# A decode transformer block on Trainium2: the first load issued as two halves of 64 partitions, from two engines

## The chip, the cores and the metric

The kernel runs on one core of one Trainium2 chip. The metric is the device time of one execution in microseconds; the number given is the median of several runs.

## The reference

Four sequences, one new token each (B = 4, D = 448), go through one block: layer norm, attention over a cache, output projection, residual; then layer norm twice, an MLP (448 to 1792 to 448, tanh GELU) and a second residual. Everything is float32.

```python
q = (layernorm(x) @ wq)                     # 16 heads of 256
k, v = caches[:, :, 4096 - 1024:, :]        # 8 kv heads, last 1024 positions, each used by 2 heads
p = softmax(q @ k.T * 256 ** -0.5)
h = x + (p @ v) @ wo
y = layernorm(layernorm(h))
out = h + gelu(y @ w1 + b1) @ w2 + b2
```

## The kernel before, in words

The work on the cache is split into eight groups, one per kv head. Of each group the kernel needs the query weights (128 rows by 1792 floats once packed), the keys and the values (128 by 8192 floats each), and the output weights (128 by 1792). Nearly all bytes are used once, so the kernel is a stream of large loads through two rings of two buffers each, with the compute behind them.

**Ring "k"** holds the keys of a group and, in the same load, the query weights of the next group. **Ring "v"** holds the values of a group and its output weights. The very first load is different: it takes a buffer of ring "v" for the query weights of group 0 together with `xT`, the token `x` transposed to 128 partitions by 4 chunks by 4 sequences (16 floats per partition). In all it is 1808 floats in each of 128 partitions, 904 KB. The second load (`k0`, line 69) is the keys of group 0 and three quarters of the query weights of group 1; the last quarter of those comes as two small transfers (`wq1_last`, line 73). After that come, in this order, keys 1, values 0, keys 2, values 1 and so on, and at the end the MLP weights `w1` and `w2` through ring "k".

All these loads are issued by SyncE (SP), from the helper `load` (line 48; the DMA is line 52). ScalarE issues four small DMAs (line 132): the rows of `x`, `b1` and `b2` in another layout, 11 KB in all as the profile counts them. They write the tile `rs`, which GpSimd clears first (line 130), behind its clearing of `qT`, `oT`, `pT` and `gT` (line 127).

**The path from the first load.** TensorE takes column means of `xT` (lines 138 and 139), VectorE centres it (148) and squares it (268), TensorE and VectorE take the variance (138, 139, 141, 152), GpSimd the power -0.5 (153), VectorE writes the normed token `yT` (271 to 273), TensorE projects it with the query weights of group 0 (159), ScalarE copies the result (161), TensorE transposes it (165), VectorE folds it (167) and writes `qT` (173). Then `scores` of group 0 can start on the keys (182). Later steps on the same engines: VectorE maxima (186), ScalarE exponentials (194), TensorE transposes of the probabilities (207), values (219), the transposed output (240) and its sum over groups in `acc` (248).

**What sets the order.** TensorE's instructions run in the order of the program text. Those of the other engines are put in order by a scheduler at build time, which also places the waits: a load into a ring's buffer waits until the last reader of the buffer's former contents is done. Completions of loads are counted on eight counters, handed to the loads in the scheduler's order, so each load also waits for the landing of the load that had its counter eight loads earlier.

Of the kernel before, what the change touches and what calls it, by code (L numbers as in the profile page):

```python
# [8 lines left out]
F32 = mybir.dt.float32  # L9
# [6 lines left out]
B, D = 4, 448  # L16
# [4 lines left out]
P = 128  # L21
H = P // 2
ND = 4
# [4 lines left out]
CACHE = NKC * B * DH  # L28
WEIGHTS = 4 * D
# [4 lines left out]
def block_kernel(ctx: ExitStack, tc, rows, wq0, k0, wq1, kq, vo, w1, w2, out):  # L34
    nc = tc.nc
    const = ctx.enter_context(tc.tile_pool(name="const", bufs=1))
    ring = ctx.enter_context(tc.tile_pool(name="ring", bufs=2))
# [10 lines left out]
    def load(kind, src, pieces, name):  # L48
        t = ring.tile([P, CACHE + WEIGHTS], F32, tag=kind, name=name)
        at = 0  # L50
        for n in pieces:
            nc.sync.dma_start(t[:, at : at + n], src[:, at : at + n])  # L52
            at += n
        return t


    def wq_parts(t, last=None):
        parts = [(a, yT[:, a, :], slice(0, 512), t[:, a * 512 : (a + 1) * 512]) for a in range(3)]
        if last is not None:
            return parts + [(3, yT[:H, 3, :], slice(0, 512), last)]  # L60
        for i in range(2):
            parts.append((3, yT[:, 3 + i, :], slice(i * 2 * P, (i + 1) * 2 * P), t[:, 3 * 512 :]))
        return parts
# [195 lines left out]
        return pool.tile([P, 2, DH], F32, tag=tag, name=f"po{g}")  # L259


    t = load("v", wq0, (WEIGHTS + ND * B,), "wq0")
    wqt = wq_parts(t[:, :WEIGHTS])
    xT = t[:, WEIGHTS : WEIGHTS + ND * B].rearrange("p (a b) -> p a b", a=ND)
    d = work.tile([P, ND, B], F32, tag="d", name="d_x")
# [31 lines left out]
    t = load("k", w1, (2 * F, F + F // 2), "w1")  # L297
    w1t = [t[:, a * F : min((a + 1) * F, 3 * F + F // 2)] for a in range(ND)]
    t = load("k", w2, (8 * D, 4 * D, 2 * D), "w2")
# [127 lines left out]
    for c in range(first, NFC):  # L427
        for j in range(4):
            m, n = (Q, 2) if c == first else (B, 2 if j < 3 else 1)
# [75 lines left out]
```

## Time and profile before

| | us |
|---|---|
| median of 3 runs | 214.59 (214.48 to 214.62) |
| span of the profiled execution, first to last instruction | 212.9 |
| median less span | 1.69 |

The profile gives a span but no device time of its own for the profiled execution, so the median stands for it: 1.69 us lie outside the span, before the first or after the last instruction. Columns of the profile's tables are explained where its lines are shown. PE is TensorE, PEld its weight loads, DVE VectorE, ACT ScalarE, POOL GpSimd, SP SyncE; a q behind an engine's name is its DMA issuing. L52 is line 52 of the kernel. A row such as `0.73 0.39 SPq L52` gives start and duration in microseconds from the span's start.

### The profile page before, as it was taken

The numbers are of one execution on the slowest core, as the hardware profiler recorded it, in microseconds if no ns is written. First come the engines' busy times: TensorE is split into PE (matmuls) and PEld (weight loads), VectorE is DVE, ScalarE is ACT, GpSimd is POOL, SyncE is SP. The second block draws the span as 40 slices with busy tenths as digits, with TensorE's granted clock in tenths as the row PEclk, the third lists the DMA queues.
The fourth block names the chain that finished last, engine by engine and source line by source line (L and its number), as shares of the span: only waits on it lengthen the run. The fifth ranks groups of instructions, "written<-read, shape, count | busy, mean of one in ns | idle before, by whom it ended". The sixth has DMA issues, their size and how long they took to land.

```text
span 212.9 us, 2306 instructions
## 1 busy us (share of the span) xinstructions
PE 137.9 (65%) x971; PEld 49.1 (23%) x971; DVE 39.2 (18%) x167; ACT 21.0 (10%) x52; POOL 5.6 (3%) x17
## 2 busy tenths in 40 slices
PE   0456868093886739583986348382948476798994
PEld 0322233021231212211231113120222123234432
DVE  1420324001130202210130104110230231022320
ACT  0210213000030000300030003000030001000311
POOL 6100000000000000000000000000000000000110
PEclk9999999669597966969599859979797999699999
DMA  7999998999989999999999999999989999999991
GB/s 291 426 399 469 398 465 378 459 465 390 458 378 465 465 390 458 398 446 465 390 458 405 443 465 386 465 413 428 461 375 468 440 428 390 417 418 433 424 390 60
DMA packets 3865, 88.46 MB, mean 415 GB/s; under 512 B 448, under 2 KB 576, under 8 KB 1168
## 3 DMA queue, kind: packets, MB, share of 16 engines
q1 hardware_dynamic: 3824, 88.29, 96.9%
q8 instruction: 7, 0.11, 0.2%
q10 hardware_dynamic: 32, 0.05, 0.1%
q14 instruction: 2, 0.02, 0.0%
HBM read 88.26 MB, written 0.07 MB: 415 GB/s over the span
## 4 chain that ended last, share of the span: by engine, by line
DMA 85%; PE 11%; DVE 2%; issue 0%; SPq 0%
DMA v<-vo 65%; DMA w<-w 12%; DMA k<-k 8%; PE po L219 8%; PE acc L248 1%; DVE o L236 1%; PE pot L240 1%; PE py L431 1%; DVE oT L243 0%; DVE oT L244 0%; SPq L52 0%; DVE res L437 0%; PE py L256 0%
## 5 line engine op out<-in xcount | busy, mean ns | idle before, releaser
L182 PE MATMUL s<-k,qT 128*32 128x512 f32 x256 | 42.3, 822 | 24.7 <-DMA k<-kq 22.6
L219 PE MATMUL po<-v,pT 128*32 128x512 f32 x256 | 40.0, 772 | 19.6 <-DMA v<-vo 19.6
L186 DVE TENSOR_REDUCE mx<-s 128x1 f32<-128x512 f32 x16 | 11.1, 691 | 67.4 <-PE s L182 67.4
L182 PEld LDWEIGHTS s<-k,qT 128*32 128x32 f32 x256 | 10.0, 146 | 54.7 <-issue 29.4
L219 PEld LDWEIGHTS po<-v,pT 128*32 128x32 f32 x256 | 10.7, 135 | 42.3 <-issue 31.4
L161 ACT COPY qs<-pq 128x512 f32<-128x512 f32 x8 | 4.7, 586 | 135.8 <-PE pq L159 135.8
L236 DVE TENSOR_SCALAR o<-po,rec 128x512 f32<-128x512 f32 x8 | 6.0, 750 | 60.2 <-PE po L219 60.2
L194 ACT ACTIVATE p<-s,nm 128x512 f32<-128x512 f32 x16 | 10.9, 690 | 18.4 <-DVE nm L190 18.4
L207 PE MATMUL ppt<-ident,p 128*128 128x128 f32 x64 | 10.5, 286 | 2.0 <-ACT p L194 1.7
L165 PE MATMUL pqt<-ident,qs 128*128 128x128 f32 x32 | 5.7, 304 | 6.2 <-ACT qs L161 6.2
L240 PE MATMUL pot<-ident,o 128*128 128x128 f32 x32 | 5.2, 286 | 5.7 <-DVE o L236 5.7
L248 PE MATMUL acc<-v,oT 128*32 128x448 f32 x56 | 6.7, 551 | 3.3 <-DVE oT L244 3.3
L207 PEld LDWEIGHTS ppt<-ident,p 128*128 128x128 f32 x64 | 6.7, 140 | 6.0 <-ACT p L194 6.0
L159 PE MATMUL pq<-k,yT 128*32 128x512 f32 (+1 forms) x66 | 7.3, 515 | 0.0
L308 PE MATMUL warm<-idle 128*32 128x512 bf16 x25 | 7.3, 382 | 0.0
L240 PEld LDWEIGHTS pot<-ident,o 128*128 128x128 f32 x32 | 3.3, 140 | 13.0 <-DVE o L236 13.0
L165 PEld LDWEIGHTS pqt<-ident,qs 128*128 128x128 f32 x32 | 3.6, 150 | 10.9 <-ACT qs L161 9.1
L153 POOL TENSOR_TENSOR r<-ve_r,mhalf 128x1 f32<-128x1 f32 x2 | 1.1, 544 | 191.9 <-DVE ve_r L152 191.9
L211 DVE COPY pT<-ppt 128x16 f32<-128x16 f32 x32 | 4.7, 170 | 4.7 <-PE ppt L207 4.7
L159 PEld LDWEIGHTS pq<-k,yT 128*32 128x32 f32 x66 | 3.1, 110 | 6.1 <-issue 4.8
L138 PE MATMUL pm_x<-wq,mean 128*128 128x12 f32 x2 | 0.6, 363 | 5.8 <-DMA wq<-wq 5.8
L167 DVE TENSOR_REDUCE sm<-pqt 128x16 f32<-128x64 f32 x8 | 1.8, 225 | 13.0 <-PE pqt L165 13.0
(101 smaller groups left out, 60.9 us busy)
## 6 DMA issues: line engine op xcount, KB each, us to landing
v<-vo SPq DMA_DIRECT2D x7, 4992.0 KB, 31.8
k<-kq SPq DMA_DIRECT2D x6, 4992.0 KB, 32.0
k<-k SPq DMA_DIRECT2D x1, 4864.0 KB, 16.3
k<-kq SPq DMA_DIRECT2D x1, 4096.0 KB
w<-w SPq DMA_DIRECT2D x2, 1792.0 KB
v<-vo SPq DMA_DIRECT2D x2, 1024.0 KB, 22.2
v<-vo SPq DMA_DIRECT2D x1, 2048.0 KB
w<-w SPq DMA_DIRECT2D x1, 1344.0 KB
```

The costliest lines, as they stand in the source:

```text
L159: nc.tensor.matmul(pq[j * Q : (j + 1) * Q, cols], y, w, start=True, stop=True)
L161: nc.scalar.copy(qs, pq)
L165: nc.tensor.transpose(pt[:, i, :], qs[:, i * P : (i + 1) * P], ident)
L182: nc.tensor.matmul(s[b * Q : (b + 1) * Q, :], qT[g % 2][:, c, b, :], kt[h][:, c, b, :], start=(c == 0), stop=(c == 1),)
L186: nc.vector.reduce_max(mx[:, h : h + 1], s, axis=AX.X)
L194: nc.scalar.activation(p[:, h * 512 : (h + 1) * 512], halves[h], AF.Exp, bias=nm, scale=SCALE, accum_out=sums[:, h : h + 1],)
L207: nc.tensor.transpose(pt[:, c, :], p[:, (4 * h + c) * P : (4 * h + c + 1) * P], ident)
L219: nc.tensor.matmul(po[b * Q : (b + 1) * Q], pT[g % 2][:, c, b, :], vt[c][:, :, b, :], start=(c == 0), stop=(c == NKC // 2 - 1),)
L236: nc.vector.tensor_scalar_mul(o, po, rec)
L240: nc.tensor.transpose(pt[:, i, c], o[:, i, c * P : (c + 1) * P], ident)
L248: nc.tensor.matmul(acc[i * Q : (i + 1) * Q, :], oT[g % 2][:, i, :], wt[:, i, :], start=(g == 0), stop=(g == HKV - 2),)
L308: nc.tensor.matmul(warm[:Q], idle[:, :Q], idle, start=True, stop=True)
```

## The change

The first load no longer goes through `load`. Its tile is taken from ring "v" as before, and its 1808 columns are loaded in two DMAs: partitions 0 to 63 issued by SyncE, partitions 64 to 127 issued by ScalarE. Nothing else differs in the text.

```diff
-    t = load("v", wq0, (WEIGHTS + ND * B,), "wq0")
+    t = ring.tile([P, CACHE + WEIGHTS], F32, tag="v", name="wq0")
+    n = WEIGHTS + ND * B
+    for q, rows_half in ((nc.sync, slice(0, H)), (nc.scalar, slice(H, P))):
+        q.dma_start(t[rows_half, :n], wq0[rows_half, :])
     wqt = wq_parts(t[:, :WEIGHTS])
```

Here `P` is 128, `H` 64, `WEIGHTS` 1792, `ND * B` 16.

## The prediction

> **What bounds the kernel now.** I first read the top of the page: the span, the busy slices, the queues, the chain.
>
> ```profile
> span 212.9 us, 2306 instructions
> ...
> DMA  7999998999989999999999999999989999999991
> ...
> q1 hardware_dynamic: 3824, 88.29, 96.9%
> ...
> HBM read 88.26 MB, written 0.07 MB: 415 GB/s over the span
> ...
> DMA 85%; PE 11%; DVE 2%; issue 0%; SPq 0%
> ```
>
> The sixteen DMA engines are busy in all forty slices but the first and the last, SyncE's queue (q1) alone fills 96.9% of them, and 85% of the chain that ended last is transfers. The first question is whether the stream is short of work anywhere, so I read the stretches. The columns are length, the five engines' busy time, TensorE's clock, DMA share, GB/s.
>
> ```profile
> 1.60:2.60 1.00, 0.00 (x0) 0.00 (x0) 0.02 (x1) 0.00 (x0) 1.00 (x5) 1.00 0.70 137
> 1.60:9.60 8.00, 2.20 (x8) 2.00 (x8) 1.31 (x9) 1.28 (x1) 2.85 (x8) 1.00 1.05 424
> 9.60:21.40 11.80, 6.84 (x34) 2.43 (x38) 2.47 (x16) 0.59 (x1) 0.62 (x1) 1.00 1.01 431
> 21.40:208.40 187.00, 127.13 (x877) 43.30 (x869) 34.30 (x139) 18.88 (x50) 1.09 (x2) 0.85 1.00 427
> ```
>
> From 1.6 to 208.4 us the stream runs at 424 to 431 GB/s. The first microsecond of data looks slow (137 GB/s, share 0.70), but the first 8 us together reach 424: the deficit against 431 is 8.0 x 7/431 = 0.13 us. So the end of the kernel is start of data + bytes / rate + a tail, and an early change counts by how far it moves the stream. To see how far ahead of the data the issues are, I read the chain in order of time:
>
> ```profile
> 1.18 16.26 DMA k<-k
> ...
> 17.46 24.74 DMA v<-vo
> ...
> 50.74 38.90 DMA v<-vo
> ...
> 182.14 26.22 DMA w<-w
> ...
> 210.21 0.29 DVE res L437
> ```
>
> The values issued at 50.74 land 38.90 us later: several loads lie queued ahead of them. In the steady part the queue never runs dry, and the chain is the queue.
>
> For the start alone I read the DMA share from 0 to 6 us, in slices of 0.15 us:
>
> ```profile
> DMA  0000000000099016497699999596999999960009
> ```
>
> The first packets come in the twelfth slice, at 1.65 us, followed by a thin half microsecond and then a full stream.
>
> **The change, part by part.** These are the rows of the first 25 us, from the timeline.
>
> ```profile
> 0.73 0.39 SPq L52 DMA_DIRECT2D wq<-wq  x1
> ...
> 1.18 0.41 SPq L52 DMA_DIRECT2D k<-k  x1
> ...
> 1.22 0.29 POOL masks.py:199 TENSOR_SCALAR_AFFINE_SELECT ident<-ident 128x128 f32<-128x128 f32 x1
> ...
> 1.63 1.55 SPq L73 DMA_DIRECT2D wq_last<-wq  x2
> ...
> 3.35 0.69 POOL L130 MEMSET rs<- 128x704 f32 x1
> 4.07 1.54 ACTq L132 DMA_DIRECT2D rs<-rows  x4
> 5.64 1.28 ACT L161 ACT_TABLE_LOAD   x1 [5.64 <-issue]
> 5.68 0.34 SPq L52 DMA_DIRECT2D k<-kq  x1
> ...
> 5.80 0.57 PE L138 MATMUL pm_x<-wq,mean 128*128 128x12 f32 x2 [5.80 <-DMA wq<-wq]
> ...
> 8.94 0.17 DVE L152 TENSOR_SCALAR ve_x<-cm_sx 128x4 f32<-128x4 f32 x1
> 9.01 0.18 DVE L102 TENSOR_TENSOR sel<-ident 128x32 f32<-128x32 f32 x1
> ...
> 13.62 0.59 ACT L161 COPY qs<-pq 128x512 f32<-128x512 f32 x1 [6.69 <-PE pq L159]
> ```
>
> ```profile
> 15.73 0.25 DVE L173 COPY qT<-sm 128x16 f32<-128x16 f32 x2
> 17.46 0.33 SPq L52 DMA_DIRECT2D v<-vo  x1
> ...
> 17.58 5.82 PE L182 MATMUL s<-k,qT 128*32 128x512 f32 x32 [2.15 <-DMA k<-k]
> ...
> 24.29 0.33 SPq L52 DMA_DIRECT2D k<-kq  x1
> 24.72 0.38 SPq L52 DMA_DIRECT2D v<-vo  x1
> ```
>
> Bytes. 904 KB before, twice 452 KB after: 0 us of transfer. At 427 GB/s the whole first load is 926 KB (decimal) / 427 = 2.2 us of the stream.
>
> SyncE's issue. One full issue took 0.39 us. The half's issue is not in the trace; the issues in these rows run from 0.33 to 0.41 us for 128 partitions, and ScalarE's four small ones took 1.54/4 = 0.39 us, so I see no price by rows and take 0.39. Bounds for the issue of k0: 0.06 us earlier to 0.02 later. Even that isn't felt, since the half ahead of it is still being moved: 0 us.
>
> ScalarE's added issue. Estimate 0.39 us from those four, at about 0.8 us, when ScalarE has nothing else: its first DMA comes at 4.07, after GpSimd's clearing of rs. Cost 0. This holds if the scheduler puts the new DMA ahead of the four, which stand earlier in the text but are not ready. The rows of VectorE show that it does such things: line 102, whose input GpSimd had finished by 1.51 us, is behind lines 141 to 152. If the cover is gone (the new DMA behind the four, at 5.6 us), see the second rival.
>
> The start of the data. With two queues the thin first microsecond could fill, or stay. Bounds: a gain of 1.00 x (427 - 137)/427 = 0.68 us if it became a full one and everything behind it moved up, against 0.13 us by the 8 us row, which shows that the thin start is mostly made good by 9.6 us. I take 0, nearest to the 8 us row, and keep -0.68 as the far end.
>
> Moved waits. The load issued at 5.68 (keys 1) is the ninth in the scheduler's order (first load, k0, four rows, two wq_last, then keys 1) and waits for the first one's landing; the tenth (values 0, at 17.46) waits for that of k0. These are the queue's own waits:
>
> ```profile
> SPq L52 <- DMA k<-k: 11.4, 1, 11.4
> ...
> SPq L52 <- DMA wq<-wq: 2.5, 1, 2.5
> ```
>
> With one load more, and ScalarE's half second in order, the ninth is the second wq_last, which then waits for SyncE's half; the tenth, keys 1, waits for ScalarE's half; values 0 still waits for k0, and all later pairs stay as they are. Behind the waiting wq_last on SyncE stands keys 1. Cost: SyncE's two small issues take 1.55/2 = 0.78 us each, so keys 1 goes out at about 5.63 + 0.78 = 6.4 us instead of 5.68. What hides it is k0, still moving until 17.44; the first packets of the first load came 0.9 us after its issue (0.73 to 1.65), so keys 1 is late only beyond 17.44 - 0.9 = 16.5 us. Hidden by 10 us: 0.
>
> The landing of x. If ScalarE's half starts a little later than SyncE's, packets of k0 come between its own and it lands late. The chain from landing to qT runs from 5.80 to 15.73 + 0.25 = 15.98, and TensorE then waits for k0 until 17.58: 1.6 us of slack before scores move at all. Beyond that, scores release keys 2 at 24.29, while values 0 are in transfer until 42.20; issue may slip by 42.20 - 0.9 - 24.29 = 17 us. So even a landing at 15 us costs the stream nothing; I price it at 0, with far end 0. A faster landing gains nothing for the same reason: TensorE would wait for k0 longer.
>
> Half width. A DMA into 64 partitions isn't in the trace. Its bounds: below, no loss, as the rest of the stream; above, half the rate while one half moves alone, 463 KB / 427 = 1.1 us lost. Both halves are issued within 0.1 us of each other and queue together, which is nearest to one load of 128: I take 0.
>
> [...]
>
> **Sum.** Against the profiled execution: 212.9 + 0 (bytes) + 0 (issues) + 0 (start, -0.68 to 0) + 0 (half width, 0 to +1.1) + 0 (waits) = 212.9 us, plus the 1.69 outside the span: 214.59, rounded 214.6, the median of the runs shown.
>
> **The rivals.**
>
> First, faster: the start fills. For it: share 0.70 and 137 GB/s in the first microsecond, and VectorE, TensorE and ScalarE idle there, so nothing else is late. Against: 424 GB/s over 8 us. It gives between 214.59 - 0.13 = 214.5 and 214.59 - 0.68 = 213.9; only its far part is over 0.2%.
>
> Second, slower, and the change not doing what it says: the new DMA is ordered behind the four of line 132. It is then issued at 4.07 + 1.54 = 5.6 us, not at the start, and becomes the seventh in the counters' order, so the tenth load, keys 1, waits for the second, k0, and is issued at 17.46. The point from which it decides is 16.5 us, above. The queue is then empty from the last packet of k0 until 17.46 + 0.9 = 18.4. At least 0.9 us is lost. By bytes, the first load and k0 are 5.9 MB, done on the average engine at 1.6 + 5.9 MB / 427 = 15.4 us, so at most 18.4 - 15.4 = 3.0 us. Nearest is the slowest engine, which ends at about 17.4: I take 1.5 and get 216.1 (215.5 to 217.6). For it: the four stand earlier in the text, and ScalarE works in order. Against: VectorE's line 102, which shows an order by readiness.
>
> Third, slower: half width. If each half goes to its partitions at half rate and they don't overlap, +1.1 us: 215.7. [...] Against the price: with both in flight all partitions are being written, and k0 follows at once.
>
> **How the numbers follow.** A time of no change (within 0.2%, 0.43 us, about what a measurement can tell from no change) 0.74: 214.6, its own range 214.2 to 215.0. Start fills 0.10, of which 0.08 beyond 0.43 us. Second rival 0.10. Half width or an unseen cost of two queues taking turns 0.06. Faster 0.08, same 0.76 (with the near part of the first rival), slower 0.16. The range reaches from 214.1 to 215.7: it leaves out the far end of the start and most of the second rival.
>
> **What would show it.** In the profile after: an ACTq issue of the first load at about 0.8 us, ahead of the four; keys 1 issued between 6 and 8 us and anyhow before 16.5; values 0 at about 17.5; the stretch 1.6 to 9.6 at about 424 GB/s; the chain's last w landing near 208.4. The forecast is wrong if the four rows precede the half and keys 1 goes out after 16.5 with a gap in the DMA share near 17 us, or if the first stretch is clearly above 431 (faster) or below 400 GB/s (half width).

## The result, and the profile after

The changed kernel takes 216.97 us (median of 4 runs, 216.47 to 217.28), against 214.53 for the kernel before on the same chip: the ratio is 1.0113, with a 95% interval of 1.0101 to 1.0125. It is slower by 2.44 us. The forecast was no change, 214.6, with a range up to 215.7.

The top of the page of the changed kernel:

```profile
span 215.5 us, 2307 instructions
...
DMA  6999999999999999999999999999999998999991
...
q1 hardware_dynamic: 3760, 87.82, 95.9%
q10 hardware_dynamic: 112, 0.51, 1.0%
...
DMA 86%; PE 10%; DVE 2%; issue 0%; SPq 0%
```

The DMA engines are as busy as before, and transfers still make the chain. ScalarE's queue, q10, now carries 0.51 MB. Where the time went is seen from the stretches (length, the engines' busy time, TensorE's clock, DMA share, GB/s):

```profile
1.60:9.60 8.00, 1.12 (x5) 1.03 (x5) 0.54 (x4) 1.28 (x1) 2.45 (x7) 1.00 1.05 315
9.60:21.40 11.80, 5.00 (x26) 2.56 (x30) 3.12 (x19) 0.59 (x1) 1.03 (x1) 1.00 0.99 417
21.40:208.40 187.00, 126.48 (x877) 42.53 (x869) 34.21 (x138) 18.31 (x47) 1.09 (x2) 0.86 1.00 429
```

From 21.4 us on the rate is the same (429 GB/s, 427 before). The loss lies ahead of that: 8.0 x (424 - 315)/427 = 2.04 us in the first stretch and 11.8 x (431 - 417)/427 = 0.39 in the second, 2.43 together. These rows count a packet whole in the stretch in which it starts. With packets shared out at the border, the trace's packet records give 0.94 MB less than before at 21.4 us, which is 2.2 us, and the stream is still 2.2 us behind at 200 us. The DMA share is 1.05 in both kernels' first stretch: the engines are not idle, they move fewer bytes while busy. This is the line to notice: **the same busy share of 1.05 stood beside 424 GB/s before and beside 315 now**.

The timeline of the start, and then the loads that the prediction spoke of:

```profile
0.73 0.57 SPq L265 DMA_DIRECT2D wq<-wq  x1
0.74 0.56 ACTq L265 DMA_DIRECT2D wq<-wq  x1
...
1.37 0.83 SPq L52 DMA_DIRECT2D k<-k  x1
...
2.25 4.13 SPq L73 DMA_DIRECT2D wq_last<-wq  x2
...
4.08 1.51 ACTq L132 DMA_DIRECT2D rs<-rows  x4
...
7.67 0.34 SPq L52 DMA_DIRECT2D k<-kq  x1
...
7.79 0.57 PE L138 MATMUL pm_x<-wq,mean 128*128 128x12 f32 x2 [7.79 <-DMA wq<-wq]
...
17.72 0.25 DVE L173 COPY qT<-sm 128x16 f32<-128x16 f32 x2
20.38 0.33 SPq L52 DMA_DIRECT2D v<-vo  x1
```

Both halves go out at once, and ScalarE's stands ahead of its four small loads, as forecast. But x lands at about 7.7 us instead of 5.7, and k0 lands at 20.37 instead of 17.44 (its landing releases the values' issue). The last weights, and the last add with them, are late by about as much as the stream was at the start:

```profile
1.37 19.00 DMA k<-k
...
184.84 26.00 DMA w<-w
...
212.70 0.29 DVE res L440
```

The end of the weights moves from 208.36 to 210.84, 2.48 us. The 0.2 to 0.3 us above the 2.2 of the stream come up at its end; why is open.

The DMA view of the changed kernel from 1.6 to 3.5 us has one queue in it:

```profile
DMA packets 52, 0.38 MB, mean 198 GB/s; under 512 B 0, under 2 KB 0, under 8 KB 52
...
q10 hardware_dynamic: 52, 0.38, 88.0%
```

and from 3.5 to 6.2 us nearly all bytes are SyncE's, on q1:

```profile
q1 hardware_dynamic: 82, 0.81, 122.2%
q10 hardware_dynamic: 28, 0.09, 13.3%
```

So the halves went **one after the other**, ScalarE's first, although they were issued within 0.01 us. SyncE's half, issued at 0.73, took 6.9 us to land (the last figure of this row of the DMA view), so it is the one that x and keys 1 wait for:

```profile
wq<-wq SPq DMA_DIRECT2D x1, 452.0 KB, 6.9
```

The packet records of the trace give the size of it: the 128 rows of 7232 B are 128 packets in both kernels; before, half of them took 274 ns or less (the median), now the median is 507 ns.

### The profile page after: what moved, and what is told of

Read it like the earlier page. It is cut to its first block, busy times and chain, and to the rows that moved or that the text cites. A ratio compares the mean times of both kernels' runs of the same rounds, so it can differ in the third digit from the quotient of the medians.

```text
span 215.5 us, 2307 instructions
## 1 busy us (share of the span) xinstructions
PE 136.4 (63%) x971; PEld 47.9 (22%) x971; DVE 39.2 (18%) x167; ACT 21.0 (10%) x52; POOL 5.6 (3%) x17
## 4 chain that ended last, share of the span: by engine, by line
DMA 86%; PE 10%; DVE 2%; issue 0%; SPq 0%
DMA v<-vo 65%; DMA w<-w 12%; DMA k<-k 9%; PE po L219 7%; PE acc L248 1%; DVE o L236 1%; PE pot L240 1%; PE py L434 1%; SPq L265 0%; DVE oT L243 0%; DVE oT L244 0%; DVE res L440 0%; PE py L256 0%
## 5 line engine op out<-in xcount | busy, mean ns | idle before, releaser
L182 PE MATMUL s<-k,qT 128*32 128x512 f32 x256 | 43.7, 845 | 27.2 <-DMA k<-kq 24.1
L219 PE MATMUL po<-v,pT 128*32 128x512 f32 x256 | 36.2, 714 | 18.7 <-DMA v<-vo 18.5
L219 PEld LDWEIGHTS po<-v,pT 128*32 128x32 f32 x256 | 9.2, 127 | 39.8 <-issue 25.9
```

What stands on the lines that cost most here:

```text
L182: nc.tensor.matmul(s[b * Q : (b + 1) * Q, :], qT[g % 2][:, c, b, :], kt[h][:, c, b, :], start=(c == 0), stop=(c == 1),)
L219: nc.tensor.matmul(po[b * Q : (b + 1) * Q], pT[g % 2][:, c, b, :], vt[c][:, :, b, :], start=(c == 0), stop=(c == NKC // 2 - 1),)
```

## The experiments

**The theory** is half width: a DMA that writes only partitions of one half of the 128 moves at about half rate (the median packet above takes 507 ns where it took 274), and the halves don't overlap. Twice the 1.1 us of the prediction's third rival makes 2.2 us. The first packets are also 0.30 us later: the first busy slice of the DMA row from 0 to 6 us begins at 1.95 us instead of 1.65.

```profile
DMA  0000000000000998379789998539299099899929
...
1.60:2.60 1.00, 0.00 (x0) 0.00 (x0) 0.02 (x1) 0.00 (x0) 1.00 (x5) 1.00 0.77 181
```

Whether that adds to the loss is not shown. The microsecond from 1.6 us moves more than before (181 GB/s, 137 before), and at 2.8 us both kernels have moved 0.2 MB by the packet records.

**The rivals**: the second queue costs the time (two queues taking turns); the moved waits do (keys 1 waits for SyncE's half and goes out at 7.67 instead of 5.68); what counts is the number of partitions of a DMA and not which.

The diffs below are cut to the lines that tell the runs apart. Where the first load is in halves or in three parts of the partitions, the run starts from the changed kernel, else from the kernel before.

### Both halves on one queue

```diff
-    for q, rows_half in ((nc.sync, slice(0, H)), (nc.scalar, slice(H, P))):
+    for q, rows_half in ((nc.sync, slice(0, H)), (nc.sync, slice(H, P))):
```

> Both halves of 64 partitions are issued by SyncE; nothing goes to ScalarE's queue. Theory, half width: packets into one half of the partitions move at half rate (in the profile of the changed kernel they take about 500 ns, against 274 ns before), the halves go one after the other, so 926 KB cost twice 926 KB / 427 GB/s = 2.2 us: +2.2 us, about 216.7, as in the changed kernel. Rival, two queues: the loss comes from the second queue (ScalarE's); with one queue it goes: 214.5. Rival, moved waits: the order of the counters is as in the changed kernel (keys 1 waits for the second half): 216.9 as well.

Measured: 216.94 us, ratio 1.0112 (1.0095 to 1.0129). The loss stays without ScalarE's queue. The second queue is not the cause. The first stretch again is busy and slow (351 GB/s at a DMA share of 1.10):

```profile
1.60:9.60 8.00, 1.58 (x6) 1.49 (x6) 1.10 (x9) 1.28 (x1) 2.45 (x7) 1.00 1.10 351
```

### Two queues, halves of the columns

```diff
+    for q, cols in ((nc.sync, slice(0, n // 2)), (nc.scalar, slice(n // 2, n))):
+        q.dma_start(t[:, cols], wq0[:, cols])
```

> SyncE and ScalarE each issue half of the columns (904 floats) of all 128 partitions. Theory, half width: all partitions are written by each DMA, so packets run at full rate: 214.5, within 0.3 us. Rival, two queues: 216.9 as in the changed kernel. Rival, moved waits: the extra load shifts the counters in the same way, 216.9.

Measured: 214.68 us, ratio 1.0005 (0.9996 to 1.0014), with the first stretch back at full rate:

```profile
1.60:9.60 8.00, 2.21 (x8) 2.00 (x8) 1.48 (x10) 1.28 (x1) 3.05 (x8) 1.00 1.06 428
```

Same two engines, same number of loads, same bytes, all partitions in each: no loss. Together the two runs point to the partitions as the cause, and clear both the second queue and the one load more.

### The same cut on a larger load

If it is the width, the cost goes with the bytes. The load of keys 4, in the middle of the kernel, has 5.11 MB; the first load is as before. In this and two later runs the parts differ:

```diff
-            t = load("k", kq[g - 1], pieces, f"k{g}")
+            if g == 4:
+                t = ring.tile([P, CACHE + WEIGHTS], F32, tag="k", name=f"k{g}")
+                for q, r in ((nc.sync, slice(0, H)), (nc.sync, slice(H, P))):
+                    q.dma_start(t[r, :], kq[g - 1][r, :])
```

> The first load is as before. The load of keys 4 (5.11 MB, in the middle of the kernel) is issued by SyncE as two halves of 64 partitions, one after the other. Theory, half width: cost goes with the bytes, 5.11 MB / 427 GB/s = 12.0 us lost: 226.5. Rivals, two queues or a cost of the start of the kernel: 214.5 to 215.

Measured: 230.9 us, ratio 1.0776 (1.0745 to 1.0807), +16.4 us. The direction and the scale are the theory's, the size is over it. The stretches of this kernel around the load:

```profile
60.00:85.00 25.00, 15.45 (x105) 5.30 (x102) 4.36 (x19) 2.86 (x7) 0.00 (x0) 0.86 1.00 430
85.00:116.00 31.00, 9.21 (x56) 2.85 (x54) 2.27 (x12) 1.01 (x4) 0.00 (x0) 0.71 1.01 211
...
130.00:200.00 70.00, 47.79 (x308) 14.83 (x304) 11.43 (x45) 5.32 (x14) 0.00 (x0) 0.81 1.00 430
```

211 GB/s is half of 430, with a DMA share of 1.01. Lost are 31 x (430 - 211)/430 = 15.8 us of the 16.4. The packet records show why it is more than the 12.0 expected. From 86.9 to 116.2 us 146 packets of 39936 B take over 2.2 us each, where 1.48 is usual: the 128 of the load and 18 of its neighbours, 0.7 MB. Their mean is 3.23 us, more than twice 1.48, and 146 x (3.23 - 1.48)/16 engines = 16.0 us. Why neighbours are slowed too is open.

The control cuts the same load in two halves of the columns:

```diff
+            t = load("k", kq[g - 1], ((CACHE + WEIGHTS) // 2,) * 2 if g == 4 else pieces, f"k{g}")
```

> The load of keys 4 is issued by SyncE as two halves of the columns, all 128 partitions in each: the control of the two tests on keys 4. Theory: every part writes all partitions, no cost: 214.5, within 0.3 us. Rival: cutting a load in two costs something by itself: up to 231.

Measured: 214.7 us, ratio 1.0009 (0.9999 to 1.0018). Cutting by itself costs nothing that these runs can tell.

### Which partitions, or how many

The parts are now partitions 32 to 95, 0 to 31 and 96 to 127, all by SyncE. The first is again a DMA of 64 partitions with the same bytes.

```diff
+                for q, r in ((nc.sync, slice(Q, 3 * Q)), (nc.sync, slice(0, Q)), (nc.sync, slice(3 * Q, P))):
```

> The load of keys 4 (5.11 MB) is issued by SyncE in three parts: partitions 32 to 95 (half of the bytes), then 0 to 31, then 96 to 127. Theory, half width in the sense that what counts is which half of the 128 partitions a DMA writes: the middle part lies in both halves and runs at full rate, the two outer parts lie in one half each and run at half rate, so about half of the cost of the two halves of 64 (16.4 us): +8 us, 222.5. The packets of 39936 B take about 1.5 us in the middle part and 3.1 us in the outer ones. Rival: what counts is the number of partitions of a DMA (64 instead of 128): then all three parts are slow, +16 us or more, 231.

Measured: 224.37 us, ratio 1.0456 (1.0435 to 1.0477), +9.9 us. In stretches of 5 us:

```profile
85.00:90.00 5.00, 2.12 (x16) 1.29 (x19) 1.17 (x9) 1.14 (x4) 0.00 (x0) 0.89 0.93 399
...
95.00:100.00 5.00, 1.61 (x12) 0.58 (x12) 0.79 (x3) 0.00 (x0) 0.00 (x0) 0.92 0.98 203
100.00:105.00 5.00, 0.00 (x0) 0.00 (x0) 0.00 (x0) 0.00 (x0) 0.00 (x0) 0.50 0.97 200
...
110.00:115.00 5.00, 4.37 (x24) 1.09 (x28) 0.66 (x1) 0.00 (x0) 0.00 (x0) 0.50 0.93 399
```

The packet records say the same: median 1.48 us up to 92.5 us, as anywhere in the stream, then 2.9 to 3.1 us until 107.5, and 1.48 again from 110. 81 packets are slow, the 64 of the outer parts and 17 neighbours, with a mean of 3.10 us: 81 x (3.10 - 1.48)/16 = 8.2 us of the 9.9. One slow stretch of about 15 us in place of 31: the middle 64 partitions ran at full rate (1.48 us a packet), the outer two parts at half rate (203 and 200 GB/s). So for this load it was not the number of partitions of a DMA: the halves have 64 as well, and there the slow packets took a mean of 3.23 us, against 1.48 in the middle part. It was whether they lie in one half. The middle part also reads one unbroken piece of 64 rows of the source, as a half does. The same parts on the first load:

```diff
+    for q, rows_half in ((nc.sync, slice(Q, 3 * Q)), (nc.sync, slice(0, Q)), (nc.sync, slice(3 * Q, P))):
```

> The first load (926 KB) is issued by SyncE in three parts: partitions 32 to 95, then 0 to 31, then 96 to 127. Theory: half of the bytes at full rate, half at half rate, +1.1 us, and up to 0.35 us for the later start seen with the halves: 215.6 to 216.0. Rival, number of partitions: all at half rate or worse, 216.9 or more.

Measured: 216.64 us, ratio 1.01 (1.0083 to 1.0117), +2.13 us, well over the 1.1 to 1.5 expected. By its time this run doesn't tell the two apart. Its packet records do: the middle part comes first in the queue, and the packets that start from 2.8 to 3.8 us take 274 ns (median), those from 4.1 to 5.8 us 462; with both halves on SyncE's queue it was 475 and 534 ns in these stretches. Its three issues take longer, and k0 goes out at 2.49 us instead of 1.18:

```profile
0.73 1.72 SPq L265 DMA_DIRECT2D wq<-wq  x3
2.49 0.42 SPq L52 DMA_DIRECT2D k<-k  x1
```

Its first stretch has a DMA share of 0.97, against 1.05 before, so part of its loss is idle engines. How much the later issue took and how much the width was not tried separately.

### The waits

Two runs leave out two of the four small row loads, so that keys 1 no longer waits for a counter (half of the columns of the residual and the biases then stay zero). First on the changed kernel:

```diff
-    for j in range(4):
+    for j in range(2):
         nc.scalar.dma_start(rs[j * Q : j * Q + B, :], rows[j])
```

> The changed kernel with two of the four small row loads left out (so half of the columns of the residual and of the biases stay zero). Keys 1 is then the eighth load and waits for no counter. Theory, half width: the loss is in the packets, it stays: 216.9. Rival, moved waits (keys 1 waits for ScalarE's half and goes out at 7.7 us): the loss goes: 214.5.

Measured: 216.92 us, ratio 1.0113 (1.0098 to 1.0128). Keys 1 goes out at 3.82 us, and nothing is gained. The moved waits are not the cause.

```profile
3.82 0.73 SPq L52 DMA_DIRECT2D k<-kq  x1
```

Where that wait does decide is seen when ScalarE issues the whole first load:

```diff
+    nc.scalar.dma_start(t[:, :n], wq0[:, :])
```

> The whole first load is one DMA of 128 partitions issued by ScalarE; SyncE begins with k0. Theory, half width: 214.5, within 0.4 us (the first packets may come 0.3 us later, as in the changed kernel). Rival, two queues: if ScalarE's queue itself is slow or the two take turns, k0's large packets come between those of the first load, x lands late, but the stream loses only what the turns cost: 215 to 217.

Measured: 217.85 us, ratio 1.0153 (1.0138 to 1.0168), +3.3 us: against the theory's 214.5, so something else acts here. The timeline and SyncE's waits of this run:

```profile
17.98 0.34 SPq L52 DMA_DIRECT2D k<-kq  x1
18.09 0.57 PE L138 MATMUL pm_x<-wq,mean 128*128 128x12 f32 x2 [18.09 <-DMA wq<-wq]
```

```profile
SPq L52 <- DMA wq<-wq: 15.2, 1, 15.2
```

The packet records show why: from 3.8 us to the end of both loads the engines move packets of 7232 B (274 ns, full rate) in turn with k0's of 38912 B (1439 ns). x lands with the end of k0, keys 1 waits for it, and the queue runs empty:

```profile
9.60:21.40 11.80, 2.20 (x8) 2.00 (x8) 0.87 (x6) 0.00 (x0) 0.00 (x0) 1.00 0.79 308
```

11.8 x (431 - 308)/427 = 3.4 us. The same kernel with two row loads left out:

> As the run in which ScalarE issues the whole first load, but two of the four small row loads are left out (so half of the columns of the residual and of the biases stay zero). Keys 1 is then the seventh load and waits for no counter. Theory for that run's loss of 3.3 us: x lands at 18 us because its packets take turns with k0's larger ones, and keys 1 waits for it with the queue empty; here keys 1 goes out within the first 5 us, so the loss goes: 214.5 to 214.9, although x lands as late as before. Rival: the late x or ScalarE's queue costs the time itself: 217.8.

Measured: 215.26 us, ratio 1.0038 (1.0024 to 1.0053). x is as late (18.04 us), and 2.6 of the 3.3 us are gone. The wait was most of it. The 0.7 us that stay are not explained. They come up at the end: by the packet records the stream is no more than 0.1 us behind the kernel before from 25 to 200 us, and the last weights land at 208.73 us instead of 208.36.

### The halves of keys 4 on two queues

```diff
+                for q, r in ((nc.sync, slice(0, H)), (nc.scalar, slice(H, P))):
```

> The load of keys 4 in two halves of 64 partitions, one by SyncE, one by ScalarE. Theory, half width: the half in SyncE's queue follows whole loads and costs half of the 16.4 us, 8 us; the half in ScalarE's queue takes turns with packets of whole loads, which write the other half too, and costs between 0 and 8 us: 223 to 231, middle 227. If two queues with the two halves ran side by side at full rate, it would cost nothing: 214.5.

Measured: 241.43 us, from 235.32 (the profiled execution) to 244.51. Even the lowest is above the expected range; two queues make it worse, not better (230.9 with both halves on one). From 60 to 80 us of the profiled execution both queues are at work, from about 64 us on at half rate (second block, the stretches):

```profile
DMA packets 149, 5.29 MB, mean 264 GB/s; under 512 B 16, under 2 KB 16, under 8 KB 16
...
q1 hardware_dynamic: 99, 3.31, 57.2%
q10 hardware_dynamic: 49, 1.96, 44.8%
```

```profile
70.00:80.00 10.00, 7.53 (x44) 1.90 (x43) 1.10 (x3) 0.00 (x0) 0.00 (x0) 0.76 0.98 212
...
110.00:120.00 10.00, 6.70 (x44) 1.81 (x44) 1.10 (x3) 0.00 (x0) 0.00 (x0) 0.71 0.96 217
```

A whole load's packets beside the half's don't bring the rate back: 212 GB/s for both together. They are slowed themselves: beside the 64 packets of ScalarE's half, 59 of whole loads on q1 take over 2.2 us, with a median of 2.9 in both queues. SyncE's half then has a second slow stretch, 217 GB/s from 110 to 120 us. So the cost is paid on more than the load's own bytes. Why the four executions differ by 9 us stays open.

## Why the prediction was wrong, point by point

- **What bounds the kernel** was right: the stream, and an early change counts by how far it moves the stream. The 2.2 us lost before 21.4 us (2.43 by the rows) come out at the end.
- **Bytes: 0 us of transfer** was wrong as a sum, for the reason of the next point.
- **Half width** is the step that failed. The prediction took 0 because both halves "queue together, which is nearest to one load of 128", with 1.1 us as the far end. In the trace they don't run together: q10 alone until 3.5 us, then nearly all q1 (0.81 of 0.90 MB from 3.5 to 6.2 us). The far end was too small as well: it counted the loss of one half, "while one half moves alone", and both move alone, so 2 x 1.1 = 2.2 us, which is what the stream is behind by the packet records. Whether halves that ran together would lose nothing is not shown; a half and whole loads on the other queue moved 212 GB/s together. The third rival had the mechanism and its condition, at 215.7 and a chance of 0.06 (shared with two queues taking turns). The half rate in the 1.1 us was the author's estimate: no row of the kernel before shows it, and no run shows a loss of 1.1 us. What the runs showed in its place is 2.44 us for the first load, a median packet of 507 ns for 274, 211 GB/s in place of 430 with keys 4 in halves, and full rate (1.48 us a packet) for partitions 32 to 95, which lie in both halves.
- **The start of the data** was bounded by a gain alone. The first packets came 0.30 us later. That this cost time is not shown: the first microsecond moved more than before (181 GB/s, 137 before). With half width alone the sum is 2.2 us against 2.44 measured; adding 0.30 would give 2.5, and no run separates the two.
- **Issues**: that the halves' issue shows no price by rows was wrong in the trace (0.57 us, and k0 from 1.37 to 2.20 where it took 1.18 to 1.59). No run here shows that it cost anything.
- **ScalarE's issue ahead of its four small loads** was right (0.74 us), so the second rival didn't come about in the changed kernel. Its mechanism, keys 1 issued after 16.5 us, was shown by the run with the whole load on ScalarE: 2.6 us by the two runs' difference, within its 0.9 to 3.0.
- **Moved waits** were right as 0: 216.92 without the wait, 216.97 with it. The order was read the wrong way round: keys 1, at 7.67, waited for SyncE's half (0.73 + 6.9 us), and the second `wq1_last`, at 5.7, for ScalarE's. That keys 1 still fell between 6 and 8 us was luck.
- **The landing of x** was right as 0 in the changed kernel: qT is ready at 17.97, k0 lands at 20.37.
- **The start fills**, the first rival, didn't happen even where it could: two queues with halves of the columns give 214.68.

The bad choice was at one place. An unknown with ends 0 and 1.1 us was set to 0 by what the two issues look like (0.01 us apart), and here issue times didn't tell whether transfers overlap: the halves of the columns, both issued at 0.73 us, ran side by side, those of the partitions, issued at 0.73 and 0.74, one after the other.

## What to carry to other kernels

Cut a load by columns and not by halves of the partitions: a part that lies in one half of the 128 partitions moved at half the rate here (211 GB/s in place of 430), and the loss grew with its bytes (2.4 us for 0.93 MB, 16.4 us for 5.11 MB, part of that on its neighbours), while halves of the columns cost nothing that the runs can tell (ratios 1.0005 and 1.0009). In a stream-bound kernel read bytes per second by stretch beside the busy share, since the engines looked fully busy at half rate here (a DMA share of 1.01 at 211 GB/s). And count what waits for a load's landing apart from its data: in the run with the whole first load on ScalarE it took turns with k0, landed with k0's end and held back the issue of keys 1 to 17.98 us.

## What the runs showed of the hardware that was not expected

- The two halves, issued within 0.01 us on two queues with packets of equal size, went one after the other (q10 first). The two halves of the columns, also of equal packets and issued together, ran side by side (from 2.85 to 4.1 us 75 packets of q1 and 65 of q10 start), and a load of 7232 B packets took turns with one of 38912 B packets. What decides between these was not tried.
- A load into one half of the partitions slowed whole loads near it: 18 packets of neighbours in one run, and 59 packets of whole loads beside a half on the other queue in another, at 212 GB/s for both queues together.
- The issue of a 64-partition half of the first load took 0.57 us, that of all 128 partitions 0.39.
